# An FFT filter gated with a state-space scan: warm-up, small steps off VectorE, a fifth mirrored pair of row groups, and a new order

## The chip, the cores and the metric

The kernel runs on one core of a Trainium2 chip. The metric is the device time of one execution in microseconds (us), lower is better. Three runs of the kernel before took 306.59 to 307.20 us, with a median of 306.85 us.

A core has five engines that run side by side. TensorE (PE in the profile, and PEld for its weight loads) multiplies matrices into PSUM. VectorE (DVE), ScalarE (ACT) and GpSimd (POOL) do elementwise work, and SyncE (SP) here does nothing but issue DMA transfers. Each engine takes its instructions strictly in the order of its own queue, so an instruction that waits holds back everything behind it.

## The reference

`x` has 2048 rows (positions) of 1024 features. Two branches are computed from it and mixed by a gate of one number per row.

```python
g = sigmoid((x * gate_w).sum(-1, keepdims=True))
a = irfft2(rfft2(x) * (w_r + 1j * w_i))              # over all 2048 x 1024
# b: a diagonal state-space model over the 2048 positions
Lam_bar = exp(dt * Lam);  B_bar = ((Lam_bar - 1) / Lam)[:, None] * Bmat
h[t] = Lam_bar * h[t-1] + B_bar @ x[t]               # 1024 complex states
b = 2 * real(h @ Cmat.T) + x * Dskip
return g * a + (1 - g) * b
```

## The kernel before

**The filter branch** does its Fourier transforms as matrix products. `load_x` brings in `x`, `turn` transposes row groups on TensorE (`pt`, L938, against the permuting identity `ident_g`), `turn_out` copies them to `xQ` (L947), and `fold` adds and subtracts halves on VectorE (`preT`, `sums`, L961 to L972) so that the products that follow are smaller. A row group is a value of `j` from 0 to 15. The first four go one at a time and the other twelve in pairs, which makes the groups n = 0 to 9 of the tuple `MIRROR` (n = 5 is the pair j = 6, 7). In a group that is not mirrored, the forward transform along the features takes four products L445 and four wide ones L455 per row group. In a mirrored group, the odd half is first reversed by one product with an exchange matrix (`ps_r`, L988), VectorE then adds and subtracts it (L994, L995), the even half is split once more (L970, L971, L972 in place of L968), and the transform is made of the narrower products L442, L445 and L451. The results go to DRAM and come back turned (L495, L523), are transformed along the positions (L609), multiplied by the weights on VectorE (`times_w`, L632 to L637), and transformed back (L648, L662, L670, L681, L825, L829, L844 to L865).

The column of frequency zero does not fit into that scheme. `middle` computes it by itself in a chain of about twenty very small steps that pass from engine to engine: `Wrev` (L547), `Bcol` (L562, L563), `Zp` (L572), `Zr` (L577, L582), `Q` (L584 to L587), `Qb` (L590, L591), the product `qps` (L594) and `Qn` (L597). ScalarE writes `Qn` into the first column of each `X2` (L620), which L632 multiplies. `unit_cols` (L625) puts ones into the first column of the weights.

**The scan branch** works in eight chunks of 256 positions. For each, TensorE makes B x into `psu` (L410, 32 products per block of 128 states), ScalarE casts it to `h` (L420), and VectorE does a two-level scan: products with tables of powers (L340, L343), joins (L346, L349), `fold` (L362), the scan instruction itself (L368), then ScalarE scales (L372, into `su` or `xQ`), VectorE adds (L376), and a last pair of products and joins (L340, L343, L383, L387) gives the states. The first two chunks are done in two halves each (`NSEP`), with tiles of half the size and `su` in place of `xQ`. TensorE then makes `ps_y` (L732, and `ps_q` L746 in the last chunk) from `h` and the transposes of C (`CT`, loaded by L721). The tables of powers `tab` are made by `make_tab` in four passes: angles (L281 on ScalarE or L283 on VectorE, chosen per block of states by the tuple `ANG_ACT`), sine and cosine, and casts on all three elementwise engines (L289 to L306).

**The order of the work** is written by hand. Every part is a generator, and each letter of the string `ORDER` advances one of them by one step. `PIECES` gives the order of the pieces of the scans, and `SLOTS` the PSUM buffer of each product. Each engine's queue follows from that. Three more constants matter here. `WARM` is the number of products of zeros (`psw`, L1005) that `keep_warm` puts at the head of TensorE's queue; they need only the tile `idle` (a part of `A1_4`), which VectorE clears (L1000). `FILL_T` says how many transposes of the identity that nobody reads (L936) stand before the transposes of a row group. `ident_g` (L218) is a copy of the identity that the iota-like mask of GpSimd makes.

Of the kernel before, what the change touches and what calls it, by code (L numbers as in the profile page):

```python
# [57 lines left out]
ORDER = (
    "xTUffxxVVTTUGaTffGV2VVVG|far|xaFEUffFfUttxaTTfFSTktxx2TfEUUfttUAfUSAEaTwFEffafTrtfttStUFFEfUtTffbFEA",
    "fSUf~uF2TUEbttxxUUSArU1EASSUAAtSFEFbbbbbttbAtffget~frbEutttbbhHtbftttS1FEbffbtttbAb~tt1t1ut11hHSvAFE",  # L60
    "ftvhH~urrrr1tFF1vStKcEeScccctckf11AvvEtvccvvtthhthvhttthttvcHttetttcct1tAHHHtvvvcfeHFEvwvvvvvSvtvtSv",
    "ttvvvvvvFvvvwvvcccvvvvvvEwcA11hSSA1AK1hAe1KKKKsYsYshsHsHsHhhvvvvvvvMLnWHvvvnvNJnvvvsNJnvvvvssvsvMMvv",
    "sshsvNvYsHLyyNs3hs44vvvvHhWHMvmm+j5535M44MJnMW6nnH3Mvvvm7v7N5vJvv+vn5WvM4N8856hvhvJm4vvJ7vWY+Wvj5H3N",
    "J7vN5H44h56y8v+j8m+YHhM377H8v54ymWn84556vNndvvvhJMvv5M3M5N77nn+5dvhvvvvYy6hvvvv8m+vm445WHJJNNmdM37Mh",
    "87vHJH558+mv44j6v8YMy77n83YX+mJHNnJ8+vv554+y4m56vN5nvY5v5hv768yv7vNvmnvv877v+mvvJHhJH8+8vqhvvYiivmhq",
    "qiii+yvmNIIvqniYHHvIvii+IvIIvvvvvIqJqnqiIvIiIvvm+mNNJJvvvvvnviIivi%nI+vNvvvvvIyvqiIhXYNiivvHIhIlHJlp",
    "phlzJzlZXZPPzzhZZZZHRRHRRRRppZZZZdmyPZo+ROvZvlQQlQoooDzvDmOvvPlQBvvRvBzZZZv++vpOBDDYlOvoZPZZQRRQvRRR",
    "zzRBDvZpPloOlCZDzovZZZOvZoYDzvBBvooYYQZZoZZRZRDQZ9RooDQRRyR9C00yDDD9C99Q09900D00",
# [76 lines left out]
def kernel(  # L145
# [72 lines left out]
    nc.vector.tensor_copy(out=ident_g.rearrange("p (g s) -> p g s", g=2), in_=ident.rearrange("p (s g) -> p g s", g=2))  # L218
# [314 lines left out]
    def middle():  # L533
# [38 lines left out]
        nc.vector.tensor_copy(out=Zp, in_=zps.rearrange("p c b -> p b c"))  # L572
# [50 lines left out]
    def unit_cols():  # L623
        for p in range(4):
            nc.vector.tensor_copy(out=fft["Wb"][p % 2][:, :, :, 0], in_=unit_w.unsqueeze(2).to_broadcast([P, 2, 4]))  # L625
            yield
# [612 lines left out]
```

## Time and profile before

| what | value |
|---|---|
| median of three runs | 306.85 us |
| the profiled execution: time, span | 306.91 us, 305.1 us |
| PE busy, instructions | 294.8 us (97%), 2464 products |
| DVE busy, instructions | 289.2 us (95%), 374 |
| ACT busy, instructions | 207.0 us (68%), 309 |
| POOL busy, instructions | 72.0 us (24%), 106 |
| first product, first copy of `xQ` on VectorE | 1.90 us, 5.65 us |
| last matmul ends, last VectorE instruction ends | 300.34 us, 300.72 us |

The span is what the profiler saw between the first and the last instruction of that execution; 1.8 us of the time lie around it. A row of the groups gives line, engine, operation, tiles and count, then the busy time in us, the mean duration of one in ns, and the idle time of the engine just before these instructions with the engine that ended it. A row of the chain of waits gives the start, the length and the instruction. A row of the timeline gives the start, the busy time, and the engine, followed by the instruction and, in brackets, the idle time ahead of it. A row of the windows gives the busy time of each engine within a stretch of time, and after the letter x the number of instructions.

### The profile page before, as it was taken

How to read it: one execution, taken by the hardware profiler on the slowest of the kernel's cores; microseconds unless marked ns; L12 is line 12 of the kernel's file. 1: busy time of each engine (PE TensorE's matmuls, PEld its weight loads, DVE VectorE, ACT ScalarE, POOL GpSimd, SP SyncE). 2: the span in 40 equal slices, each digit the busy share in tenths (PEclk: the TensorE clock that was granted, in tenths of full speed). 3: DMA queues.
4: the chain of work that ended last, by engine and by line, in shares of the span. 5: the costliest groups of instructions: out<-in, count | busy, mean ns of one | idle time of the engine just before them, and what ended most of it. 6: DMA issues, size and time to landing. Idle time of an engine off the chain costs nothing.

```text
span 305.1 us, 6248 instructions
## 1 busy us (share of the span) xinstructions
PE 294.8 (97%) x2464; PEld 195.4 (64%) x2464; DVE 289.2 (95%) x374; ACT 207.0 (68%) x309; POOL 72.0 (24%) x106
## 2 busy tenths in 40 slices
PE   7989999999999999999999999999999999999993
PEld 4555687886884584467564763688567995465442
DVE  3999999999989999999999999999999999999993
ACT  1699999897541385958886888856979866393200
POOL 1133155393710002110202112120102033351430
PEclk9999999999999999999999999999999999999999
DMA  7999996999994977899989868998659726999796
GB/s 236 367 210 195 202 227 190 105 208 154 217 247 82 259 174 145 201 261 280 212 220 216 213 163 206 236 245 248 179 167 210 145 26 124 156 175 187 104 142 227
DMA packets 74140, 59.21 MB, mean 194 GB/s; under 512 B 44872, under 2 KB 61664, under 8 KB 74112
## 3 DMA queue, kind: packets, MB, share of 16 engines
q1 hardware_dynamic: 66560, 49.69, 64.6%
q0 software_dynamic: 6896, 8.69, 23.2%
q10 hardware_dynamic: 656, 0.44, 0.4%
q8 instruction: 19, 0.31, 0.4%
q14 instruction: 9, 0.07, 0.1%
HBM read 27.33 MB, written 23.08 MB: 165 GB/s over the span
## 4 chain that ended last, share of the span: by engine, by line
PE 68%; DVE 21%; ACT 5%; issue 3%; DMA 2%; POOL 0%; SPq 0%; POOLq 0%; ACTq 0%; DVEq 0%
PE ps_y L732 24%; PE psu L410 23%; PE ps_q L746 7%; DVE h L368 3%; DVE h L343 2%; PE ps_id L829 2%; DVE xQ L947 2%; DMA xs<-in_A_x_dram 2%; DVE UV L632 1%; ACT ZT L690 1%; PE ps_is L681 1%; PE ps_id L825 1%; PE ps_s L474 1%; PE ps_fd L455 1%; PE ps_s L609 1%
## 5 line engine op out<-in xcount | busy, mean ns | idle before, releaser
L410 PE MATMUL psu<-xQ,BT 128*128 128x256 bf16 x1024 | 115.7, 273 | 0.4 <-ACT A_last L489 0.3
L410 PEld LDWEIGHTS <-BT 128*128 128x128 bf16 x1024 | 99.3, 98 | 16.4 <-issue 3.8
L732 PE MATMUL ps_y<-CT,h 128*128 128x512 bf16 x416 | 93.5, 379 | 0.7 <-ACT ye L763 0.4
L732 PEld LDWEIGHTS <-h 128*128 128x128 bf16 x416 | 39.8, 98 | 48.8 <-issue 3.9
L804 POOL DMA_DIRECT2D y_scratch<-su x20 | 17.8, 953 | 127.3 <-ACT su L798 95.3
L420 ACT CAST h<-psu 128x1024 bf16<-128x1024 f32 x32 | 32.1, 1013 | 17.4 <-PE psu L410 12.5
L343 DVE TENSOR_TENSOR h<-h,tab 128x4096 bf16<-128x4096 bf16 (+1 forms) x20 | 37.3, 1863 | 0.6
L368 DVE TENSOR_TENSOR_SCAN h<-rz,h 128x512 bf16<-128x512 f32 (+1 forms) x14 | 36.3, 2617 | 0.2
L763 ACT ACTIVATE ye<-ps_y,omg 128x512 f32<-128x512 f32 x26 | 17.4, 686 | 17.6 <-PE ps_y L732 9.9
L372 ACT ACTIVATE xQ<-h,r_sb 128x254 bf16<-128x254 bf16 x48 | 21.3, 503 | 9.1 <-DVE h L368 9.1
L340 DVE TENSOR_TENSOR xQ<-h,tab 128x4096 bf16<-128x4096 bf16 x12 | 27.4, 2281 | 0.0
L746 PE MATMUL ps_q<-CT,h 128*128 128x512 bf16 (+2 forms) x112 | 20.9, 349 | 0.0
L870 POOL DMA_DIRECT2D BT<-y_scratch x10 | 12.6, 1538 | 27.4 <-issue 23.3
L619 ACT CAST X<-ps_s 128x1024 bf16<-128x1024 f32 x16 | 16.1, 1007 | 4.3 <-PE ps_s L609 2.9
L690 ACT CAST ZT<-ps_is 128x1024 bf16<-128x1024 f32 x16 | 16.9, 1113 | 2.0 <-issue 1.2
L656 ACT CAST C<-ps_is 128x1024 bf16<-128x1024 f32 x16 | 15.6, 1010 | 3.4 <-PE ps_is L648 2.6
L836 ACT ACTIVATE BT<-ps_id,gB 128x1024 bf16<-128x1024 f32 x14 | 15.1, 1111 | 3.6 <-DMA out_dram<-BT 1.8
L746 PEld LDWEIGHTS <-h 128*128 128x128 bf16 x112 | 10.4, 98 | 10.5
L461 ACT CAST X<-ps_fd 128x1024 bf16<-128x1024 f32 x16 | 16.1, 1015 | 0.1
L798 ACT ACTIVATE su<-xs,omg 128x512 f32<-128x512 bf16 x20 | 14.0, 720 | 0.5 <-DVE xs L788 0.5
L372 ACT ACTIVATE su<-h,r_sb 128x254 bf16<-128x254 bf16 x16 | 7.0, 495 | 8.4 <-DVE Zp L572 4.6
L947 DVE COPY xQ<-pt 128x1024 bf16<-128x1024 bf16 x12 | 8.1, 682 | 3.8 <-PE pt L938 3.8
(211 smaller groups left out, 432.9 us busy)
## 6 DMA issues: line engine op xcount, KB each, us to landing
y_scratch<-ye SPq DMA_DIRECT2D x20, 256.0 KB, 2.9
y_scratch<-su POOLq DMA_DIRECT2D x20, 256.0 KB, 6.5
Bb<-turn_scratch SPq DMA_DIRECT2D x16, 256.0 KB, 4.8
turn_scratch<-C SPq DMA_DIRECT2D x16, 256.0 KB, 4.3
raw<-turn_scratch SPq DMA_DIRECT2D x8, 512.0 KB, 5.2
xs<-in_A_x_dram SPq DMA_DIRECT2D x13, 256.0 KB, 5.3
out_dram<-BT SPq DMA_DIRECT2D x11, 256.0 KB, 4.8
CT<-in_A_x_dram SPq DMA_DIRECT2D x5, 512.0 KB, 5.2
```

The source lines that it names most:

```text
L340: nc.vector.tensor_mul(out=tmps["s"], in0=u[:, :, ::-1], in1=bc(i))
L343: nc.vector.tensor_mul(out=u, in0=u, in1=bc(i))
L368: nc.vector.tensor_tensor_scan(out=seg, data0=flat(rz, i), data1=seg, initial=0.0, op0=ALU.mult, op1=ALU.add)
L372: nc.scalar.activation(out=tmps["s"][:, 0, :, i, 1:TS], in_=u[:, 1, :, i, 0:TS - 1], func=ACT.Copy, scale=r2_sb[:, js.start + i:js.start + ...
L410: nc.tensor.matmul(psu[:, j, :], lhsT=BT[4 * q + j][:, ri, d8, :], rhs=xQ[:, c, d8, :], start=(d8 == 0), stop=(d8 == 7))
L420: nc.scalar.copy(out=hs[c][:, :, ri, 4 * q:4 * q + 4].rearrange("p e b (q j) -> p e b q j", j=16), in_=psus.pop((c, q, ri)).rearrange("p b ...
L461: (nc.vector.tensor_copy if j in FD_DVE else nc.scalar.copy)(out=X1.rearrange("p r (m e c) -> p r m e c", e=2, c=2), in_=psf.pop(j).rearra ...
L690: nc.scalar.copy(out=fft["ZT"][:, kp, :, :, 2 * G:2 * G + 2], in_=pszs.pop((G, kp)).rearrange("p v (x n) -> p x n v", n=64))
L732: nc.tensor.matmul(psy, lhsT=hs[c][:, tq, ri, jb, :], rhs=CT[ri][:, jb, 512 * dh:512 * (dh + 1)], start=(i == 0), stop=(i == 15 and tb not ...
L746: nc.tensor.matmul(psq, lhsT=hs[c][:, tq, ri, jb, :], rhs=CT[ri][:, jb, at:at + n], start=(i == 0), stop=(i == 15))
L763: nc.scalar.activation(out=ye, in_=psys[tb][:, K * hf:K * (hf + 1)], func=ACT.Copy, scale=omg[:, tb:tb + 1])
L804: nc.gpsimd.dma_start(out=y_dram[tb, hf], in_=xgs[tb, hf], accum_op=ALU.add)
```

## The change

- `WARM` goes from 7 to 5, and `FILL_T` from 22 to 6 transposes.
- `ident_g` (L218) is copied by GpSimd instead of VectorE.
- All eight angle products of `make_tab` are now on ScalarE (L281); four were on VectorE (L283).
- `MIRROR` takes in group 5, so one more pair of row groups has its odd half mirrored. On TensorE this makes 20 in place of 16 L442, 44 in place of 48 L445, 40 in place of 32 L451, 24 in place of 32 L455, and 5 in place of 4 L988. On VectorE one L968 goes, and one each of L970, L971, L972, L994 and L995 comes.
- In `middle`, six copies (L547, L562, L563, L572, L582, L597) go from VectorE to ScalarE, and five steps (L584, L586, L587, L590, L591) to GpSimd; the four copies of `unit_cols` (L625) go to GpSimd.
- `ORDER`, `PIECES` and `SLOTS` are new, so the instructions of every engine are in another order.

```diff
-FILL_T = {2: 22}
-WARM = 7
+FILL_T = {2: 6}
+WARM = 5
-ANG_ACT = (4, 5, 6, 7)
+ANG_ACT = (0,1,2,3,4,5,6,7,)
-    0, 1, 3, 2, 4, 5, 6, 7, 9, 8, 10, 11, 12, 13, 14, 15, 16, 17, 18, 20, 21, 19, 22, 24, 23, 25, 26, 27, 28, 29, 30,
+    0, 1, 2, 3, 5, 6, 9, 4, 8, 10, 11, 7, 12, 13, 14, 15, 16, 18, 17, 20, 21, 22, 19, 24, 23, 25, 26, 27, 29, 28, 30,
...
-MIRROR = (6, 7, 8, 9)
+MIRROR = (5, 6, 7, 8, 9)
...
-    nc.vector.tensor_copy(out=ident_g.rearrange("p (g s) -> p g s", g=2), in_=ident.rearrange("p (s g) -> p g s", g=2))
+    nc.gpsimd.tensor_copy(out=ident_g.rearrange("p (g s) -> p g s", g=2), in_=ident.rearrange("p (s g) -> p g s", g=2))
...
-        nc.vector.tensor_copy(out=Wrev, in_=wrps)
+        nc.scalar.copy(out=Wrev, in_=wrps)
...
-        nc.vector.tensor_copy(out=Bcol[:, 0:2], in_=aps.rearrange("j (r b a) -> j r a b", r=2, a=4))
-        nc.vector.tensor_scalar_mul(out=Bcol[:, 2], in0=Bcol[:, 0], scalar1=-1.0)
+        nc.scalar.copy(out=Bcol[:, 0:2], in_=aps.rearrange("j (r b a) -> j r a b", r=2, a=4))
+        nc.scalar.activation(out=Bcol[:, 2], in_=Bcol[:, 0], func=ACT.Copy, scale=-1.0)
...
-        nc.vector.tensor_copy(out=Zp, in_=zps.rearrange("p c b -> p b c"))
+        nc.scalar.copy(out=Zp, in_=zps.rearrange("p c b -> p b c"))
...
-        nc.vector.tensor_copy(out=Zr[:, 0], in_=zrp[:, :, 0])
-        nc.vector.tensor_mul(out=Q[:, 0], in0=each(AB[:, 0]), in1=every(Zp.rearrange("p b r -> p r b")))
-        nc.vector.tensor_mul(out=Q[:, 1], in0=each(AB[:, 1]), in1=every(Zr))
-        nc.vector.tensor_add(out=Q[:, 0], in0=Q[:, 0], in1=Q[:, 1])
+        nc.scalar.copy(out=Zr[:, 0], in_=zrp[:, :, 0])
+        nc.gpsimd.tensor_mul(out=Q[:, 0], in0=each(AB[:, 0]), in1=every(Zp.rearrange("p b r -> p r b")))
+        nc.gpsimd.tensor_mul(out=Q[:, 1], in0=each(AB[:, 1]), in1=every(Zr))
+        nc.gpsimd.tensor_add(out=Q[:, 0], in0=Q[:, 0], in1=Q[:, 1])
...
-        nc.vector.tensor_sub(out=Qb[:, :, 0], in0=Q[:, 0, 0, 0], in1=Q[:, 0, 1, 1])
-        nc.vector.tensor_add(out=Qb[:, :, 1], in0=Q[:, 0, 1, 0], in1=Q[:, 0, 0, 1])
+        nc.gpsimd.tensor_sub(out=Qb[:, :, 0], in0=Q[:, 0, 0, 0], in1=Q[:, 0, 1, 1])
+        nc.gpsimd.tensor_add(out=Qb[:, :, 1], in0=Q[:, 0, 1, 0], in1=Q[:, 0, 0, 1])
...
-        nc.vector.tensor_copy(out=Qn.rearrange("p b r -> p (b r)"), in_=qps)
+        nc.scalar.copy(out=Qn.rearrange("p b r -> p (b r)"), in_=qps)
...
-            nc.vector.tensor_copy(out=fft["Wb"][p % 2][:, :, :, 0], in_=unit_w.unsqueeze(2).to_broadcast([P, 2, 4]))
+            nc.gpsimd.tensor_copy(out=fft["Wb"][p % 2][:, :, :, 0], in_=unit_w.unsqueeze(2).to_broadcast([P, 2, 4]))
```

The new order is seen at three places. The first is VectorE's queue at the third of the four half chunks of the scan, from its scan L368 to its L376, which adds what ScalarE makes of that scan, and a little on. Before:

```order
L362 TENSOR_TENSOR h<-h 128x2x512
L368 SCALAR_TENSOR_TENSOR h<-rz,h 128x512 x2
L380 TENSOR_TENSOR ck<-h,rot 128x4x4
L547 COPY Wrev<-Wrev_ps 128x64
L562 COPY Bcol<-aps 32x128
L563 TENSOR_SCALAR Bcol<-Bcol 32x64
L376 TENSOR_TENSOR h<-h,su 128x2x512
```

And with the change:

```order
L380 TENSOR_TENSOR ck<-h,rot 128x4x4
L340 TENSOR_TENSOR xQ<-h,tab 128x4096
L376 TENSOR_TENSOR h<-h,su 128x2x512
L343 TENSOR_TENSOR h<-h,tab 128x4096
L349 TENSOR_TENSOR h<-xQ,h 128x2x1024
```

Three small steps of `middle` have left the stretch between the scan and its L376, and the first wide product of a whole chunk (L340 into `xQ`) stands there instead.

The second place is GpSimd's queue around the first store of `su` (L804, an accumulating DMA into the scratch array of the output), where the five steps of `Q` and `Qb` and the first two copies of `unit_cols` now stand. Before, it read:

```order
L550 TENSOR_TENSOR Wh<-Wc,Wrev 128x32
L551 TENSOR_TENSOR Wh<-Wc,Wrev 128x32
L554 TENSOR_TENSOR AB<-Wh 128x32
L555 TENSOR_TENSOR AB<-Wh 128x32
L556 TENSOR_SCALAR AB<-AB 128x64
L804 DMA y_scratch<-su 128x512 x18
```

And with the change:

```order
L556 TENSOR_SCALAR AB<-AB 128x64
L625 COPY Wb<-unit_w 128x8
L804 DMA y_scratch<-su 128x512
L584 TENSOR_TENSOR Q<-AB,Zp 128x64
L586 TENSOR_TENSOR Q<-AB,Zr 128x64
L587 TENSOR_TENSOR Q<-Q 128x64
L590 TENSOR_TENSOR Qb<-Q 128x16
L591 TENSOR_TENSOR Qb<-Q 128x16
L804 DMA y_scratch<-su 128x512 x2
L625 COPY raw<-unit_w 128x8
```

The steps of `Q` and `Qb` now stand behind one L804, which waits for an L798 of ScalarE and for a store of `ye` to land.

The third place is SyncE's queue at the loads of C (L721), and the stores of the forward transform (L495) of the tiles `A1` (A_129), `A1_last` and `A1_sc`. Before:

```order
L721 DMA_TRANSPOSE CT_82<-in_B_C_re_dram 128x8x128
L495 DMA turn_scratch<-A_129 128x2x512
L721 DMA_TRANSPOSE CT_83<-in_B_C_im_dram 128x8x128
L721 DMA_TRANSPOSE CT_82<-in_B_C_re_dram 128x8x128
L721 DMA_TRANSPOSE CT_83<-in_B_C_im_dram 128x8x128
L721 DMA_TRANSPOSE CT_82<-in_B_C_re_dram 128x8x128
L721 DMA_TRANSPOSE CT_83<-in_B_C_im_dram 128x8x128
L495 DMA turn_scratch<-A_129 128x2x512
L495 DMA turn_scratch<-A_last 128x2x512 x2
L495 DMA turn_scratch<-A_sc 128x2x512 x2
```

And with the change, to the end of these loads:

```order
L495 DMA turn_scratch<-A_last 128x2x512 x2
L721 DMA_TRANSPOSE CT_82<-in_B_C_re_dram 128x8x128
L721 DMA_TRANSPOSE CT_83<-in_B_C_im_dram 128x8x128
L721 DMA_TRANSPOSE CT_82<-in_B_C_re_dram 128x8x128
L721 DMA_TRANSPOSE CT_83<-in_B_C_im_dram 128x8x128
L495 DMA turn_scratch<-A_sc 128x2x512
L721 DMA_TRANSPOSE CT_82<-in_B_C_re_dram 128x8x128
L721 DMA_TRANSPOSE CT_83<-in_B_C_im_dram 128x8x128
L721 DMA_TRANSPOSE CT_82<-in_B_C_re_dram 128x8x128
L721 DMA_TRANSPOSE CT_83<-in_B_C_im_dram 128x8x128
L721 DMA_TRANSPOSE CT_82<-in_B_C_re_dram 128x8x128
L721 DMA_TRANSPOSE CT_83<-in_B_C_im_dram 128x8x128
L495 DMA turn_scratch<-A_sc 128x2x512
```

All sixteen loads of C stood ahead of the last five stores; now ten of the loads stand behind the stores of `A1_last`, and six of them behind the first store of `A1_sc` as well.

More of the change, by code (lines that the diff above doesn't have):

```diff
@@ L44 @@
 PIECES = (
[7 rows of a table removed]
[7 rows of a table added]
 )
 SLOTS = (
-    "0123012320132012012310210321032103201230132013201302310231012312032103131201203103203013031203120312",
-    "0312310210321021321032320310321032032031031023102310210321230120310321032",
+    "0123012310231012301230123013201320123012301202130213023102310231023102320132013320120132130132130130",
+    "13012010123012301301302302130213021301302132132310231023123103210321230123",
 )
-MIRROR = (6, 7, 8, 9)
+MIRROR = (5, 6, 7, 8, 9)
 ORDER = (
[L59 to L68, printed above, removed]
@@ new lines @@
+    "xxTU2TxffUGGVVVVVfVGaxx|aaffT22xUfTttffU|ffFFtTTEaaETtUttFkSaxEfTUxtfFTAUffSUExttfArfUbbrbtbTFSS~bFT",
+    "fUErTfuUUUUUUttfFrtbfbtbAAttFtSEESErSgAAffbffbASAhbtt~~etHuhutbFFttttttttFtffHvtwEEEbbbbSFEftttvv11t",
+    "wh~uhr1ttSSShvtKeHAFF1H1t1tArAA111ctvftt11vt~vcHfvEhhtuvfEt1vvvSttStcctHHvAAtccFFvt1vvEEvrhHvevvvv1t",
+    "SSvvchcKhhvtttvvveKKccAhvA1vnvvccwewKcvvvcvcc1KsHYshvvHHvHvWnWvvvvvvNJvvNMJnnYMvvssvvvvvvNvYssLvvyvv",
+    "vvvvvNHLJvjhHshsHssksvvmmhWW3+yHvvmnsssss44vJY+ynnvMMMM3+vN5vnvvNv5JJ5vvm4Ym645M7vMhNN73vhJj5W45y46H",
@@ new lines @@
+    "v8875vJ8MM+h3vv75H+mv458Mn6Mh4HNYW78v5v3m557Jvj8nH44vv65vMn+vvM77535Nh44vv68M8v7y+5Wmn7JNh3v55vh88HW",
+    "N6Hv+4m4HmvJYnXj7M3Jvh78544N8HvY556vJyv7++7m5mvd88+nNn55678vvN7Jvhvv+8vYdqnhHvNvHJiyvqmmIvviIvqvvhHq",
+    "++viivhIIYiiHvvvvyqymvvvIIiIqnJvvmiiqIIviIv+v+nNNvvmmivqiJnJviIivInviIIvYvYidyhNI%+yIlvhXXvvvvvzlvHJ",
+    "NHJpzPpPdZZ+hlllZZZmhZQQH+zRRvRRRzZZRZppRHDoDZRmvYlpPPZZQOovvlzvzlOvDQZBZovZZBvRRZZQQPvzDzRRvloZOvZp",
+    "vDoOoRZlZBRvDDZvBooZQDzOvvvzZZvvBOBQoPZZRoZZoRDDCYoRR90yRR90CyY+99DQDC9900oQD0090Y",
```

12 rows, old and new, of the table PIECES are left out of this document.

## The prediction

> **What bounds the kernel now.** I read the busy shares of the page first, then the windows of 10 us, then the chain of waits, and last the groups, shapes apart, for the prices.
>
> ```profile
> span 305.1 us, 6248 instructions
> PE 294.8 (97%) x2464; PEld 195.4 (64%) x2464; DVE 289.2 (95%) x374; ACT 207.0 (68%) x309; POOL 72.0 (24%) x106
> ```
>
> Both TensorE and VectorE are busy nearly all the time, so the share alone doesn't say which of them sets the end.
>
> ```profile
> core 0: us, PE busy (x) PEld busy (x) DVE busy (x) ACT busy (x) POOL busy (x), PEclk, DMA share, GB/s
> 0.00:10.00 10.00, 8.11 (x77) 5.42 (x78) 4.72 (x19) 2.22 (x7) 1.90 (x13) 1.00 0.81 270
> 20.00:30.00 10.00, 9.68 (x75) 4.96 (x76) 9.90 (x23) 9.81 (x13) 4.71 (x6) 1.00 1.14 206
> 80.00:90.00 10.00, 10.00 (x94) 8.72 (x92) 8.60 (x15) 4.69 (x7) 3.56 (x10) 1.00 0.91 225
> 210.00:220.00 10.00, 9.24 (x82) 5.95 (x81) 9.86 (x9) 9.49 (x15) 0.86 (x1) 1.00 0.63 176
> ```
>
> VectorE idles 5.3 us in the first stretch and 1.4 us at 80 to 90 us; in the other stretches shown it is 9.9 of 10 busy, and what is missing there is the step from one instruction to a dependent one. TensorE shows holes where it waits for the others, as at 210 to 220 us. A matmul that is queued behind another counts as busy, so its 97% is an upper value.
>
> ```profile
> 1.33 0.35 DVE ident_g L218
> 1.90 3.17 PE psw L1005 x7
> 5.07 0.56 PE pt L938 x8
> 5.65 0.70 DVE xQ L947
> 211.42 1.81 ACT h L420 x2
> 279.57 20.77 PE ps_q L746 x112
> 300.37 0.35 DVE raw L918
> ```
>
> The chain starts on VectorE with a copy that the throwaway products don't need but stand behind, passes through those products, and hands VectorE its first real work at 5.65 us. Around 211 us it goes from VectorE's scan through ScalarE to TensorE again, and it ends in TensorE's last products, whose inputs VectorE finished. So VectorE's queue, with no slack after 5.65 us, sets the joins, and TensorE runs from join to join with little slack of its own.
>
> **The change part by part.** The start comes first. `ident_g` leaves VectorE, so the clearing of `idle` begins right away and not after 1.33 us; five products at 3.17 / 7 = 0.45 us take 2.3 us and end near 3.3 us.
>
> ```profile
> 1.00 0.29 POOL masks.py:199 TENSOR_SCALAR_AFFINE_SELECT ident<-ident 128x128 bf16<-128x128 bf16 x1
> 0.73 1.35 SPq L247 DMA_DIRECT2D CT<-in_A_x_dram  x3
> CT<-in_A_x_dram SPq DMA_DIRECT2D x2, 256.0 KB, 2.8
> ```
>
> The identity ends at 1.29 us, and even a copy that GpSimd takes a whole microsecond for would have `ident_g` ready by 2.4 us. The first tile of `x`, issued at 0.73 us, lands 2.8 us later, at 3.5 us. From there to VectorE the chain above has 0.56 us, or 0.8 us from the first of the eight transposes if they run slowly, so VectorE begins at 4.1 to 4.5 us in place of 5.65 us. **Term one: -1.2 us**, with bounds of 0 (the second tile of `x` lands late) and -1.5.
>
> Next comes VectorE's work.
>
> ```profile
> L283 DVE TENSOR_SCALAR ang<-tau_f,ang 128x256 f32<-128x256 f32 x4 | 1.2, 343 | 0.0
> L572 DVE CAST Zp<-zps 128x32 bf16<-128x32 f32 x1 | 0.2, 162 | 0.0
> L625 DVE COPY Wb<-unit_w 128x8 bf16<-128x8 bf16 x2 | 0.4, 176 | 0.0
> L994 DVE TENSOR_TENSOR preT<-preT,ps_r 128x512 bf16<-128x512 bf16 x4 | 2.7, 680 | 0.2 <-PE ps_r L988 0.2
> L995 DVE TENSOR_TENSOR preT<-preT,ps_r 128x512 bf16<-128x512 bf16 x4 | 2.7, 687 | 0.1
> L970 DVE TENSOR_TENSOR sums<-sums 128x512 bf16<-128x512 bf16 x4 | 1.9, 483 | 0.1
> L971 DVE TENSOR_TENSOR preT<-sums 128x256 bf16<-128x256 bf16 x4 | 1.2, 292 | 0.1
> L972 DVE TENSOR_TENSOR preT<-sums 128x256 bf16<-128x256 bf16 x4 | 1.1, 282 | 0.0
> L968 DVE TENSOR_TENSOR preT<-sums 128x512 bf16<-128x512 bf16 x2 | 0.8, 416 | 0.0
> ```
>
> It loses four L283 (1.2), six copies that go to ScalarE (0.16 us for L572, 1.2 together with the slightly larger others), five steps of that kind that go to GpSimd (1.0 together) and four L625 (0.7): 4.1 us. The mirrored pair adds 0.68 + 0.69 + 0.48 + 0.29 + 0.28 and takes off one L968 of 0.42: 2.0 us. By durations that is -2.1 us, but short instructions overlap their neighbours, so I take **term two: -1.7 us**, bounds -1.2 and -2.1.
>
> The third term is the hole at 80 to 90 us, which is a wait for ScalarE.
>
> ```profile
> DVE h L376 <- ACT su L372: 1.6, 2, 1.1
> 85.74 1.70 ACT L372 ACTIVATE su<-h,r_sb 128x254 bf16<-128x254 bf16 x4 [1.10 <-DVE h L368]
> L340 DVE TENSOR_TENSOR xQ<-h,tab 128x4096 bf16<-128x4096 bf16 x12 | 27.4, 2281 | 0.0
> ```
>
> ScalarE needs 1.7 us between a scan and its L376. Before, only the small steps covered it; in the new order a 2.28 us L340 stands there. **Term three: -1.0 us** of the 1.6, bounds 0 (ScalarE is late with its own queue) and -1.6.
>
> What moves must be paid elsewhere. ScalarE takes four angle products of 0.5 us and six copies of about 0.2 us, 3.2 us in all.
>
> ```profile
> L281 ACT ACTIVATE ang<-tau_f,ang 128x256 f32<-128x256 f32 x4 | 1.8, 502 | 0.0
> ```
>
> In the first 70 us ScalarE is as full as VectorE (9.81 of 10 at 20 to 30 us), and its late casts are what TensorE and VectorE would then wait for; after that it has room (4.69 of 10 at 80 to 90 us). I put this, with the joins that VectorE now reaches earlier, into the next term.
>
> TensorE must keep up.
>
> ```profile
> L936 PE MATMUL pt<-ident 128*128 128x128 bf16 x22 | 1.4, 219 | 0.0
> L455 PE MATMUL ps_fd<-G_sb,preT 128*128 128x512 bf16 x32 | 8.2, 379 | 0.0
> L451 PE MATMUL ps_fd<-G_sb,preT 128*128 128x256 bf16 x32 | 4.8, 272 | 0.0
> L988 PE MATMUL ps_r<-preT,JP_sb 128*128 128x512 bf16 x4 | 1.5, 384 | 0.0
> ```
>
> Its first transposes start at 3.5 in place of 4.86 us (-1.4, the two products included), 16 identity transposes go (16/22 of 1.4 = -1.0), and the mirrored pair exchanges eight L455 (8.2/32 each) for eight L451 (4.8/32 each) and one L988: -0.5. That is -2.9 us of a queue that the chain shows to end at 300.34 us, if its own stalls stay: 297.4 us. The last L918 then takes 0.35 us, and the span lasts 305.1 - 300.72 = 4.4 us beyond that one: a bound of 302.2 us. VectorE's three terms alone would give 305.1 - 3.9 = 301.2 us. **Term four: +1.2 us** for the two engines meeting at tighter joins, bounds 0 and +2.5. Sum: 305.1 - 1.2 - 1.7 - 1.0 + 1.2 = 302.4 us of span, and with 1.8 us around it **304.2 us**. The profiled execution is 0.06 us above the median, which I neglect.
>
> The loads of C are the transfer at risk.
>
> ```profile
> 80.68 1.32 SPq L721 DMA_TRANSPOSE CT<-in_B_C_im_dram  x1
> CT<-in_B_C_im_dram SPq DMA_TRANSPOSE x8, 6.0
> 90.69 10.52 PE L732 MATMUL ps_y<-CT,h 128*128 128x512 bf16 x48
> ```
>
> The last one is issued at 80.7 us, takes 6.0 us to land at the median, and TensorE uses the tile from 90.7 us: 4 us to spare. Behind the stores of `A1_last` and `A1_sc`, which wait for ScalarE, I estimate from the places in the queues that the last issue comes 4 to 5 us later, and that TensorE reads the half it fills about 1 us later than the first: hidden by about a microsecond.
>
> Two rules of the Trainium skill speak against parts of this. For the start: the seven products went at 0.45 us each, where a product of that width takes 10.52 / 48 = 0.22 us later on, so the front runs at half pace although the granted clock reads 1.00 in the first window. The Trainium skill, "TensorE: Matmul & The Clock Gate" (Part 1), says that the clock opens only after a busy window of about 3.4 us that runs freely, and Part 4 that transposes don't count as busy in the same way; by that, the shorter warm-up could leave what follows at half pace for one more window. The trace, where the pace changed after 3.2 us of products, agrees so far. Rival (e) prices it from rows.
>
> For the steps on GpSimd, the rows are these (from the timeline):
>
> ```profile
> 78.27 1.23 DVE L340 TENSOR_TENSOR su<-h,tab 128x2048 bf16<-128x2048 bf16 x1
> 78.41 1.16 POOL L1035 TENSOR_SCALAR omg_bf<-g_bf 128x16 bf16<-128x16 bf16 x1
> 79.54 1.23 DVE L343 TENSOR_TENSOR h<-h,tab 128x2048 bf16<-128x2048 bf16 x1
> ```
>
> A GpSimd instruction of sixteen elements lasts 1.16 us and ends as the VectorE product ends that it began beside. The Trainium skill, "SBUF — State Buffer" (SBUF: two separate sides), says that the two engines share a pair of ports, which one takes for a whole instruction while the other stands still, VectorE with two inputs in SBUF included. By that rule the nine steps moved to GpSimd are not free: each may wait for a VectorE instruction or hold one up. Rival (b) rests on the row alone.
>
> **The rivals.** (a) TensorE takes it all back: VectorE is early, but TensorE's stalls at the joins grow by what VectorE saved, because the new order leaves less between the end of a chunk on VectorE and its first `ps_y`. For it, TensorE is as full as VectorE; against it, TensorE loses 2.9 us of work too. Then term four is +3.0 and the time 306.0 us, between 305.6 and 306.9. (b) Slower: the chain of `Q` and `Qb` on GpSimd. By my count of the queues it stands behind an L804 that is issued at about 111 us; five dependent steps, each held up by a VectorE instruction of 1.2 to 2.3 us, as L1035 above by L340, end at 112.5 us undisturbed and at 118 to 122 us if each is held up. TensorE reaches `qps` at about 116.5 us and stops there, and VectorE's L632, due at about 120.5 us, waits for `Qn` and two casts. Below 117 us nothing shows; from about 120 us on the gain is gone; at 122 us the time is 304.2 + 4.5 = 308.7 us. Against it: the 4.4 us scan L368 falls there, and one hold-up would cover several steps only if they slip in between. (c) The same on the other side: the waits of TensorE shrink too (the windows lack 0.3 us of it at 20 to 30 us and 0.8 us at 210 to 220 us), so that term four is 0 or a little less: 302.6 us. (d) C lands late: 2 us later than I estimate, TensorE and the joins lose 1 us, 305.2 us. (e) Half pace for longer in front: the eight transposes of the first tile take twice their 0.56 us, and the next tile's are hidden only in part: +0.9, 305.1 us.
>
> **How the numbers follow.** The forecast, 303.4 to 305.5 us, gets 0.48, with (d) and (e) inside it at 0.05 each; (a) 0.22; (b) 0.14; (c) 0.16. The range from 302.4 to 307.3 us leaves out the far ends of (b) and (c). A measurement here tells no change from 0.2% (0.6 us), so 306.24 and 307.46 us are the bounds. Faster takes the forecast, (c) and half of (a): 0.74. The same takes most of the rest of (a) and the low part of (b): 0.13. Slower is the rest of (b) and the tail of all: 0.13.
>
> **What would show it.** Right: VectorE's first L947 starts at 4.2 to 4.5 us; its busy time falls by about 2 us; L376's wait for `su` falls below 0.6 us; VectorE's last L918 ends near 298 us. Wrong: an L732 that waits for CT near 91 us, L632 or `qps` idle near 117 to 121 us, L586 to L591 on GpSimd lasting a microsecond each, or TensorE's idle time at the joins above the 10 us that the page now shows as missing from its span.

## The result, and the profile after

The changed kernel took 308.79 us (median of four runs, 308.29 to 309.04), and the kernel before, measured beside it, 306.94 us (306.59 to 307.20). The ratio is 1.0059, with a 95% interval of 1.0041 to 1.0077: slower by 0.6%, where I had forecast 304.2 us, and outside the range that ended at 307.3 us. The profiled execution of the changed kernel took 308.29 us, with a span of 306.5 us.

The page of the changed kernel, which answers to the two rows shown of before:

```profile
span 306.5 us, 6239 instructions
PE 295.4 (96%) x2447; PEld 195.6 (64%) x2447; DVE 287.6 (94%) x358; ACT 209.6 (68%) x319; POOL 86.8 (28%) x116
```

VectorE is busy for 1.6 us less, close to the 1.7 us of the sum. GpSimd is busy for 14.8 us more, far more than the nine small steps lasted on VectorE (1.7 us). The windows of 10 us of the changed kernel show where the time went (the columns are those of the windows before):

```profile
core 0: us, PE busy (x) PEld busy (x) DVE busy (x) ACT busy (x) POOL busy (x), PEclk, DMA share, GB/s
0.00:10.00 10.00, 7.88 (x58) 5.00 (x59) 5.44 (x21) 3.37 (x7) 1.70 (x10) 1.00 0.77 256
80.00:90.00 10.00, 10.00 (x80) 7.42 (x79) 9.78 (x12) 3.63 (x6) 0.00 (x0) 1.00 1.02 188
110.00:120.00 10.00, 7.43 (x63) 4.46 (x61) 10.00 (x7) 4.95 (x9) 7.57 (x5) 1.00 0.79 174
120.00:130.00 10.00, 8.28 (x28) 3.22 (x28) 4.83 (x3) 5.34 (x12) 3.61 (x5) 0.66 0.53 93
```

The start and the stretch from 80 to 90 us did what was forecast: VectorE is 0.7 us busier in the first and 1.2 us busier in the second. The loss is at 110 to 130 us, where next to nothing was lost before:

```profile
110.00:120.00 10.00, 10.00 (x89) 7.01 (x87) 9.81 (x11) 7.75 (x13) 1.86 (x2) 1.00 0.67 135
120.00:130.00 10.00, 10.00 (x74) 4.07 (x73) 9.96 (x6) 7.84 (x16) 0.86 (x1) 1.00 0.91 212
```

With the change, TensorE stands still for a time, VectorE idles for 5.2 us, and the granted clock falls to 0.66 on average in the second of these windows. The waits of the changed kernel name the place:

```profile
PE qps L594 <- POOL Qb L591: 4.3, 1, 4.3
DVE UV L632 <- POOL raw L625: 3.1, 1, 3.1
DVE h L376 <- ACT xQ L372: 2.5, 2, 2.2
```

This is rival (b). The timeline of the changed kernel shows its mechanism, GpSimd's five steps beside VectorE's instructions:

```profile
111.67 4.42 DVE L368 TENSOR_TENSOR_SCAN h<-rz,h 128x2048 bf16<-128x2048 f32 x1
112.28 0.96 POOL L804 DMA_DIRECT2D y_scratch<-su  x1 [11.17 <-ACT su L798]
112.98 3.23 POOL L584 TENSOR_TENSOR Q<-AB,Zp 128x64 f32<-128x64 f32 x1
116.01 2.35 DVE L340 TENSOR_TENSOR xQ<-h,tab 128x4096 bf16<-128x4096 bf16 x1
116.18 2.35 POOL L586 TENSOR_TENSOR Q<-AB,Zr 128x64 f32<-128x64 f32 x1
118.28 0.80 DVE L788 TENSOR_TENSOR xs<-xs,Db 128x1024 bf16<-128x1024 bf16 x1
118.61 0.65 POOL L587 TENSOR_TENSOR Q<-Q 128x64 f32<-128x64 f32 x1
119.00 2.40 DVE L343 TENSOR_TENSOR h<-h,tab 128x4096 bf16<-128x4096 bf16 x1
119.34 2.15 POOL L590 TENSOR_TENSOR Qb<-Q 128x16 bf16<-128x16 f32 x1
121.45 0.22 POOL L591 TENSOR_TENSOR Qb<-Q 128x16 bf16<-128x16 f32 x1
121.72 0.19 PE L594 MATMUL qps<-Qb,KRS_sb 128*128 128x32 bf16 x1 [4.29 <-POOL Qb L591]
121.94 0.19 ACT L597 CAST Qn<-qps 128x32 bf16<-128x32 f32 x1 [3.70 <-PE qps L594]
124.21 0.20 ACT L620 COPY X<-Qn 128x2 bf16<-128x2 bf16 x1
124.50 2.29 DVE L632 TENSOR_TENSOR UV<-X,Wb 128x4096 bf16<-128x4096 bf16 x1 [3.09 <-POOL raw L625]
```

The first four steps of 64 or 16 elements end within 0.2 us of the end of the VectorE instruction that they began beside: 116.21 with the scan (116.09), 118.53 with the L340 (118.36), 119.26 with the L788 (119.08), 121.49 with the L343 (121.40). The chain takes 8.7 us. TensorE, which reached `qps` at 117.4 us, waits until 121.7. Then `Qn`, two casts and two copies of the column follow on ScalarE, and VectorE's L632 starts at 124.5 us. The profile puts that wait down to L625, but the last thing before it is ScalarE's second L620, which ends at 124.4 us. A second wait of VectorE follows at 127.9 us: L376 stands for 2.2 us until L372 is done, and the clock has a part in it, as is shown below.

### The profile page after: what moved, and what is told of

It reads as the page before. It is cut to its first block, busy times and chain, and to the rows that moved or that the text cites. A ratio compares the mean times of both kernels' runs of the same rounds, so it can differ in the third digit from the quotient of the medians.

```text
span 306.5 us, 6239 instructions
## 1 busy us (share of the span) xinstructions
PE 295.4 (96%) x2447; PEld 195.6 (64%) x2447; DVE 287.6 (94%) x358; ACT 209.6 (68%) x319; POOL 86.8 (28%) x116
## 4 chain that ended last, share of the span: by engine, by line
PE 46%; DVE 42%; DMA 5%; ACT 3%; issue 2%; SPq 1%; DVEq 0%; POOL 0%; ACTq 0%
PE ps_y L732 14%; PE psu L410 14%; PE ps_q L746 7%; DVE h L343 6%; DVE h L368 5%; DVE UV L632 4%; DVE su L340 3%; DVE xQ L340 3%; PE ps_id L829 2%; DMA Bb<-turn_scratch 2%; DMA y_scratch<-su 2%; DVE xQ L947 2%; DVE h L383 2%; DVE h L349 2%; DVE h L362 2%
## 5 line engine op out<-in xcount | busy, mean ns | idle before, releaser
L732 PE MATMUL ps_y<-CT,h 128*128 128x512 bf16 x416 | 95.9, 386 | 0.0
L732 PEld LDWEIGHTS <-h 128*128 128x128 bf16 x416 | 40.4, 99 | 54.0 <-issue 10.8
L804 POOL DMA_DIRECT2D y_scratch<-su x20 | 19.5, 1035 | 73.9 <-ACT su L798 73.9
L343 DVE TENSOR_TENSOR h<-h,tab 128x4096 bf16<-128x4096 bf16 (+1 forms) x20 | 37.6, 1883 | 0.5
L368 DVE TENSOR_TENSOR_SCAN h<-rz,h 128x512 bf16<-128x512 f32 (+1 forms) x14 | 36.0, 2596 | 0.2
L763 ACT ACTIVATE ye<-ps_y,omg 128x512 f32<-128x512 f32 x26 | 17.6, 692 | 21.3 <-PE ps_y L732 17.1
L340 DVE TENSOR_TENSOR xQ<-h,tab 128x4096 bf16<-128x4096 bf16 x12 | 27.5, 2293 | 0.4 <-ACT h L420 0.3
L372 ACT ACTIVATE xQ<-h,r_sb 128x254 bf16<-128x254 bf16 x48 | 21.0, 512 | 3.5 <-DVE h L368 3.5
L798 ACT ACTIVATE su<-xs,omg 128x512 f32<-128x512 bf16 x20 | 14.3, 728 | 1.3 <-DMA y_scratch<-su 1.1
L632 DVE TENSOR_TENSOR UV<-X,Wb 128x4096 bf16<-128x4096 bf16 x4 | 9.2, 2291 | 4.7 <-POOL raw L625 3.1
L289 POOL CAST tab<-sc 128x512 bf16<-128x512 f32 x4 | 3.7, 921 | 28.9 <-ACT sc L1136 28.9
```

Of the source, the lines that this page charges most:

```text
L340: nc.vector.tensor_mul(out=tmps["s"], in0=u[:, :, ::-1], in1=bc(i))
L343: nc.vector.tensor_mul(out=u, in0=u, in1=bc(i))
L368: nc.vector.tensor_tensor_scan(out=seg, data0=flat(rz, i), data1=seg, initial=0.0, op0=ALU.mult, op1=ALU.add)
L372: nc.scalar.activation(out=tmps["s"][:, 0, :, i, 1:TS], in_=u[:, 1, :, i, 0:TS - 1], func=ACT.Copy, scale=r2_sb[:, js.start + i:js.start + ...
L632: nc.vector.tensor_mul(out=UV, in0=X2s.pop(g).unsqueeze(1).to_broadcast([P, 2, 2, 2, K]), in1=W.unsqueeze(2).to_broadcast([P, 2, 2, 2, K]))
L732: nc.tensor.matmul(psy, lhsT=hs[c][:, tq, ri, jb, :], rhs=CT[ri][:, jb, 512 * dh:512 * (dh + 1)], start=(i == 0), stop=(i == 15 and tb not ...
```

## The experiments

### Undoing one part of the chain's move, in two steps

In the first, all five steps go back to VectorE, where they fall right behind the scan L368.

```diff
-        nc.gpsimd.tensor_mul(out=Q[:, 0], in0=each(AB[:, 0]), in1=every(Zp.rearrange("p b r -> p r b")))
+        nc.vector.tensor_mul(out=Q[:, 0], in0=each(AB[:, 0]), in1=every(Zp.rearrange("p b r -> p r b")))
...
-        nc.gpsimd.tensor_sub(out=Qb[:, :, 0], in0=Q[:, 0, 0, 0], in1=Q[:, 0, 1, 1])
-        nc.gpsimd.tensor_add(out=Qb[:, :, 1], in0=Q[:, 0, 1, 0], in1=Q[:, 0, 0, 1])
+        nc.vector.tensor_sub(out=Qb[:, :, 0], in0=Q[:, 0, 0, 0], in1=Q[:, 0, 1, 1])
+        nc.vector.tensor_add(out=Qb[:, :, 1], in0=Q[:, 0, 1, 0], in1=Q[:, 0, 0, 1])
```

> The changed kernel with the five steps of Q and Qb (L584, L586, L587, L590, L591) back on VectorE; they fall between the scan L368 that ends at 116.1 us and the next L340. Theory A (this chain, held up on GpSimd, made the loss): the chain ends near 117.2 us in place of 121.7, TensorE's wait at qps falls from 4.3 to under 0.5 us, the granted clock stays at 1.00 from 118 to 126 us in place of 0.50, VectorE's idle time at 122 to 130 us (5 us) goes, VectorE does 1.0 us more work, and the time is 303.5 to 305.5 us. Theory B (the loss sits in tighter joins all along, and would come back at the next one): the wait at qps goes but the time stays above 307 us.

It took 302.67 us (301.60 to 303.06), at a ratio to the kernel before on the same chip of 0.9843 (0.9803 to 0.9883). The time fell even below the 303.5 to 305.5 us of theory A, and theory B falls. From its timeline, and the window of 120 to 130 us:

```profile
115.89 0.20 DVE L584 TENSOR_TENSOR Q<-AB,Zp 128x64 f32<-128x64 f32 x1
116.61 0.17 DVE L591 TENSOR_TENSOR Qb<-Q 128x16 bf16<-128x16 f32 x1
117.17 0.18 PE L594 MATMUL qps<-Qb,KRS_sb 128*128 128x32 bf16 x1
```

```profile
120.00:130.00 10.00, 9.84 (x78) 4.55 (x78) 10.00 (x9) 8.84 (x18) 3.53 (x3) 1.00 0.81 194
```

On VectorE the chain takes 0.9 us, not 8.7, `qps` doesn't wait, and both engines are full again. VectorE's busy time over the whole kernel is 287.7 us, against 287.6 us with the five steps on GpSimd: moving steps of 1.0 us away had saved VectorE 0.1 us. Some of its instructions beside them had been longer (L788 0.80 us against 0.68 here, L343 2.40 against 2.28).

In the second step only the three steps of `Q` are on VectorE, and the two of `Qb` stay on GpSimd.

```diff
...
-        nc.gpsimd.tensor_mul(out=Q[:, 1], in0=each(AB[:, 1]), in1=every(Zr))
-        nc.gpsimd.tensor_add(out=Q[:, 0], in0=Q[:, 0], in1=Q[:, 1])
+        nc.vector.tensor_mul(out=Q[:, 1], in0=each(AB[:, 1]), in1=every(Zr))
+        nc.vector.tensor_add(out=Q[:, 0], in0=Q[:, 0], in1=Q[:, 1])
```

> Three of the five steps (L584, L586, L587) on VectorE, the two of Qb (L590, L591) on GpSimd. Theory A: L590 is held up by the one VectorE instruction beside it (the 2.3 us L340), so Qb ends near 119.4 us, TensorE waits about 2 us at qps, its clock stays at 1.00 since the idle time is too short to close it, and the time lies about 2 us above that of the kernel with all five on VectorE, at 305.5 to 307. Theory B: no difference between the two, both above 307 us.

It took 304.68 us (303.74 to 307.41), ratio 0.9908 (0.9881 to 0.9935): 2.0 us above the first, as theory A has it, though the two intervals still touch. The time itself came out 0.8 us below the forecast range, as that of the first step did. The lines are of the slowest of its eight executions (307.41 us), the only one with a trace:

```profile
116.73 2.28 DVE L340 TENSOR_TENSOR xQ<-h,tab 128x4096 bf16<-128x4096 bf16 x1
116.90 2.20 POOL L590 TENSOR_TENSOR Qb<-Q 128x16 bf16<-128x16 f32 x1 [3.46 <-DVE Q L587]
119.07 0.66 POOL L591 TENSOR_TENSOR Qb<-Q 128x16 bf16<-128x16 f32 x1
119.78 0.18 PE L594 MATMUL qps<-Qb,KRS_sb 128*128 128x32 bf16 x1 [2.12 <-POOL Qb L591]
```

A step of 16 elements lasts as long as the L340 beside it, and TensorE waits 2.1 us. So it matters how many of the steps are on GpSimd: none, two and five of them give 302.7, 304.7 and 308.8 us.

### Held up, or slow by themselves

Here the five steps stay on GpSimd, but stand ahead of the first L804 there.

```diff
 ORDER:
-HshsHssksvvmmhWW3+yHvvmnsssss44
+HshsHsskssssvvmmhWW3+yHvvmnss44
```

The letter `s` advances the first-column chain by a step, and `+` the stores L804.

> The changed kernel with the five steps on GpSimd, but ahead of the first L804 in its queue; every other queue is as in the changed kernel. Theory A1 (GpSimd is held up by VectorE's instructions with two inputs): L584 starts at about 107.6 us and ends with a VectorE instruction, L586 waits for Zr at 111 us and is then held up, at the latest by the 4.4 us scan from 111.7 to 116.1; the last step ends at 117.5 to 121 us, and the time lies between 305 and 308.5 us. Theory A2 (these steps are slow on GpSimd by themselves, with the durations 3.2, 2.4, 0.7, 2.2 and 0.2 us that the changed kernel showed): L584 is over by 111 us and the rest ends at 111 + 5.4 = 116.4 us, TensorE does not wait at qps, and the time is 303 to 305 us. Which of the two holds is read from the ends: by A1 each step ends within 0.15 us of the end of a VectorE instruction, by A2 the durations repeat.

```profile
107.65 1.23 DVE L343 TENSOR_TENSOR h<-h,tab 128x2048 bf16<-128x2048 bf16 x1
107.81 1.25 POOL L584 TENSOR_TENSOR Q<-AB,Zp 128x64 f32<-128x64 f32 x1 [6.65 <-ACT Zp L572]
111.12 0.40 POOL L586 TENSOR_TENSOR Q<-AB,Zr 128x64 f32<-128x64 f32 x1 [2.07 <-ACT Zr L582]
111.60 0.65 POOL L587 TENSOR_TENSOR Q<-Q 128x64 f32<-128x64 f32 x1
111.99 4.53 DVE L368 TENSOR_TENSOR_SCAN h<-rz,h 128x2048 bf16<-128x2048 f32 x1
112.32 4.22 POOL L590 TENSOR_TENSOR Qb<-Q 128x16 bf16<-128x16 f32 x1
116.50 2.29 POOL L591 TENSOR_TENSOR Qb<-Q 128x16 bf16<-128x16 f32 x1
123.76 0.17 ACT L597 CAST Qn<-qps 128x32 bf16<-128x32 f32 x1
```

The durations don't repeat. L584 takes 1.25 us where it took 3.23, L586 0.40 where it took 2.35, L590 4.22 where it took 2.15, and L591 2.29 where it took 0.22, each according to the VectorE instruction beside it. The steps end up to 0.19 us behind those instructions, a little more than the 0.15 us that I had set. A1 holds and A2 falls. TensorE's wait at `qps` shrinks to 1.3 us, but the time is 306.82 us (305.98 to 307.46), ratio 0.9983 (0.9964 to 1.0003), since a new wait has taken its place: the product is done at 119.0 us, and ScalarE makes `Qn` only at 123.8 us. In ScalarE's queue `Qn` stands behind an L798 whose buffer the delayed store L804 has to free first. I had not seen that when I wrote the expectation, so it is luck that the time fell within it.

### TensorE's part and VectorE's part

In the next kernel the chain stays as in the change, and only `qps` stands sixteen products later in TensorE's queue.

```diff
 ORDER:
-yHvvmnsssss44vJY+ynnvMMMM3+vN5
+yHvvmnsssvJY+ynss44nvMMMM3+vN5
```

> The changed kernel with the product qps placed sixteen products of ps_y (3.5 us) later in TensorE's queue; the queues of GpSimd and ScalarE are the same. Qb still ends near 121.5 us. Theory A-PE (what hurts is TensorE standing still, and its clock closing): TensorE waits under 1 us, the clock stays at 1.00, TensorE gains 3.5 us of work and some 2.8 us of half pace, and the time falls to 303 to 306 us. Theory A-DVE (what hurts is VectorE waiting for Qn at L632, 3.1 us, and behind it for L376, 2.2 us): Qn is there no earlier, VectorE's idle time at 120 to 130 us stays at 5 us, and the time stays above 307.5 us.

It took 305.37 us (304.76 to 306.50), ratio 0.9944 (0.9922 to 0.9966). `Qb` comes at 121.4 us as before, TensorE waits 0.8 us, and the granted clock stays at 1.00. VectorE still starts L632 at 124.3 us, after an idle time of 3.1 us, as theory A-DVE had it, but the time falls by 3.4 us all the same. So neither theory holds alone: 3.4 of the 6.1 us between the change and the kernel with the chain on VectorE came back when `qps` stood later in TensorE's queue. What is left, 2.7 us, still has VectorE's wait of 3.1 us for `Qn` and TensorE's of 0.8 us in it, and no run parts these two.

The other kernel keeps TensorE's queue and gives it something to do while it waits: 64 throwaway products of the identity by itself, written into the tile of `qps` before `qps` is.

```diff
-        qps = psum([P, 32], "qps")
+        qps = psum([P, P], "qps")
+        for _ in range(64):
+            nc.tensor.matmul(qps, lhsT=ident, rhs=ident, start=True, stop=True)
...
```

> The changed kernel with 64 throwaway products of 128 columns (identity by identity, 3.6 us at full pace) just ahead of qps in TensorE's queue, where it otherwise stands still for 4.3 us; Q and Qb stay on GpSimd. Qb comes at 121.5 us as before. If the closing of the clock (half pace from 121 to 126.4 us) is a cost of its own, TensorE's row at 120 to 130 us shows a clock of 1.00, the first two ps_y after qps take 7.0 in place of 9.4 us, and the time falls by 1.5 to 2.5 us to 306.3 to 307.3. If the half pace was hidden by VectorE's wait for Qn, the time stays within 0.5 us of 308.8.

It took 306.24 us (305.73 to 306.99), ratio 0.9972 (0.9955 to 0.9989): 2.55 us less than the change, with `Qb`, `qps` and L632 at the same times. In the line numbers of this kernel, where L634 is the former L632 and L734 the former L732 (the last line is a window of 10 us):

```profile
117.29 3.74 PE L595 MATMUL qps<-ident 128*128 128x128 bf16 x64
121.74 0.18 PE L596 MATMUL qps<-Qb,KRS_sb 128*128 128x32 bf16 x1 [0.71 <-POOL Qb L591]
121.98 6.85 PE L734 MATMUL ps_y<-CT,h 128*128 128x512 bf16 x31
124.51 2.29 DVE L634 TENSOR_TENSOR UV<-X,Wb 128x4096 bf16<-128x4096 bf16 x1 [3.08 <-POOL raw L627]
120.00:130.00 10.00, 9.17 (x70) 4.42 (x70) 6.92 (x6) 7.21 (x15) 4.46 (x6) 1.00 0.63 122
```

The products after the wait take 6.85 us here, and in the change 9.5 us for one more of them. In the change's windows the granted clock is 1.00 until 119 us, 0.97 in the next microsecond, 0.50 from 120 to 126, 0.81 on average from 126 to 128, and 1.00 again:

```profile
119.00:120.00 1.00, 0.00 (x0) 0.00 (x0) 1.00 (x2) 0.00 (x0) 0.92 (x2) 0.97 1.00 221
120.00:121.00 1.00, 0.00 (x0) 0.00 (x0) 1.00 (x1) 0.00 (x0) 1.00 (x1) 0.50 0.74 168
121.80:124.00 2.20, 2.20 (x7) 0.79 (x7) 0.00 (x0) 2.02 (x4) 1.81 (x3) 0.50 0.54 61
124.00:126.00 2.00, 2.00 (x7) 0.62 (x5) 1.50 (x1) 1.18 (x4) 0.00 (x0) 0.50 1.03 142
```

So the clock closed during the wait of 4.3 us, and the half pace after it cost 2.55 us of its own. The way to VectorE leads through ScalarE, whose L763 waits for the slow `ps_y` and holds back the L372 behind it, for which VectorE's L376 then stands 2.2 us:

```profile
127.87 0.69 ACT L763 ACTIVATE ye<-ps_y,omg 128x512 f32<-128x512 f32 x1 [2.65 <-PE ps_y L732]
```

With the 64 products the waits of all L376 together are down from 2.5 to 0.5 us. The Trainium skill, "TensorE: Matmul & The Clock Gate" (Part 1), lets about 3.4 us without work bring half rate back. The trace shows the same effect sooner: the clock fell at 120.0 us, some 2.5 us after TensorE had stopped at 117.4. With two of the steps on GpSimd, where TensorE waits 2.1 us (from 117.7 to 119.8 us), I had expected the clock to stay open. In the profiled execution it did not, as a window of 1 us shows:

```profile
121.00:122.00 1.00, 1.00 (x4) 0.31 (x3) 0.86 (x1) 0.97 (x3) 0.94 (x2) 0.50 1.27 119
```

The granted clock is 1.00 up to 120, 0.58 in the next microsecond, 0.50 to 123, 0.72 to 124, and 1.00 again: some 3 us at half pace followed a wait of 2.1 us. That is shorter than the page's figure, and the measurement decides here. But it is not so each time. Over the whole kernel the mean granted clock was 0.993 in this execution and 0.994 in the next slowest (305.65 us), and 0.999 or 1.000 in the other six (303.74 to 305.07 us), so in most of them the clock seems to have stayed open, as expected. After the waits of 1.3 and 1.5 us in the trace of the kernel with the steps ahead of the first L804 (at `qps` and at the next `ps_y`) it stayed at 1.00. Where the bound lies, and what moves it from run to run, is open. Nor does a shorter half pace always show in the time: of the change's own four executions one had a mean clock of 0.994 and not 0.989, and took 308.59 us.

### The same move in the old order

Is it the move or the place? Here the kernel before has its five steps on GpSimd and nothing else is changed.

> The kernel before with one thing changed: the five steps of Q and Qb on GpSimd, ahead of the first L804 there. If VectorE's instructions hold the steps up in this order too, each ends with a VectorE instruction, Qb comes at about 109 to 111 us in place of 107.7, VectorE (whose Qn, L597, stands ahead of an L340) and TensorE wait 1 to 3 us, and the time is 307 to 309 us. If the steps are as quick there as the small steps L550 to L556 (0.25 us each at 86 to 87 us), VectorE saves 1.0 us and the time is 305.9 to 306.9 us.

It took 307.33 us (306.92 to 307.90), ratio 1.0005 (0.9993 to 1.0017): no change, at the low end of what the first theory gave and above the second.

```profile
106.86 0.68 DVE L376 TENSOR_TENSOR h<-h,su 128x1024 bf16<-128x1024 bf16 x1
107.02 0.70 POOL L586 TENSOR_TENSOR Q<-AB,Zr 128x64 f32<-128x64 f32 x1 [1.54 <-DVE Zr L582]
109.53 0.19 DVE L597 CAST Qn<-qps 128x32 bf16<-128x32 f32 x1 [0.53 <-PE qps L594]
```

The steps are held up here too, L586, L587 and L590 by instructions of some 0.7 us, so `Qb` comes about 1.5 us later than before, at 109.3 us. VectorE waits 0.5 us for it. It is rid of 1.0 us of steps, but its busy time stays at 289.2 us, and the time shows no gain. Here as in the change, what is left of the VectorE instruction that happens to run beside a step is its price.

### What the other parts are worth

With the chain on VectorE as the base (302.67 us, ratio 0.9843), one part at a time was undone.

```diff
 f1: front
-FILL_T = {2: 6}
-WARM = 5
+FILL_T = {2: 22}
+WARM = 7
-    nc.gpsimd.tensor_copy(out=ident_g...
+    nc.vector.tensor_copy(out=ident_g...
 f2: angles
-ANG_ACT = (0,1,2,3,4,5,6,7,)
+ANG_ACT = (4, 5, 6, 7)
 f3: the six copies of middle
-        nc.scalar.copy(out=Wrev, in_=wrps)
+        nc.vector.tensor_copy(out=Wrev, in_=wrps)
...
 g1: all of these, and L625, at once
 g3: the fifth mirrored pair
-MIRROR = (5, 6, 7, 8, 9)
+MIRROR = (6, 7, 8, 9)
```

For g3 the two letters of `ORDER` that reverse and fold group 5 and its place in `SLOTS` go as well.

> The changed kernel with Q and Qb on VectorE (the base of this set: 302.7 us), and its front undone: seven products, 22 identity transposes, ident_g copied by VectorE. If VectorE's start sets the time (the prediction's term one), its first L947 moves back by about 1.0 us to 5.6 us and the time rises by 0.8 to 1.5 us, to 303.5 to 304.2. If the start is taken up by the first waits for ScalarE or for transfers, the time stays within 0.4 us of the base.

> The base with four of the eight angle products back on VectorE (L283). If VectorE's work counts for what its durations say, the time rises by 1.2 us to 303.9. If ScalarE, which is 9.4 to 9.9 of 10 busy from 10 to 60 us in the changed kernel, is what the front waits for, the 2.0 us that it is relieved of make the time fall or stay, 301.5 to 302.9.

> The base with the six small copies of the first-column chain (L547, L562, L563, L572, L582, L597) back on VectorE. By VectorE's durations the time rises by 1.2 us, or some 0.8 us where they overlap their neighbours, to 303.5 to 303.9. A rival: on VectorE they stand behind wide instructions and come later than on ScalarE, so that the product qps waits again; then TensorE's wait there is over 0.5 us and the rise is larger, 2 us or more. Without either, no change within 0.4 us.

> The new order and the fifth mirrored pair with every step on the engine that it had before, and the old front (Q, Qb, the six copies, L625, four angles and ident_g on VectorE, seven products, 22 transposes). The three undone by themselves above the base (302.7 us) cost 0.6 for the front, 0.4 for the angles and 0.9 for the copies. If they add up, the time is 304.6 to 305.2 us, and the rest of the distance to the kernel before, some 2 us, is the new order's. If the order had been made for the new places and is of no use without them, the time is 306 us or more.

> The base (Q and Qb on VectorE, 302.7 us) without the fifth mirrored pair: VectorE does 2.0 us less, TensorE 0.5 us more. If VectorE sets the time throughout, it falls to 300.7 to 301.7 us. If TensorE sets it in the stretch where the pair falls (the first 30 us), or the two share it, the time is 302.5 to 303.5 us.

| kernel | time, us | ratio to before, 95% interval |
|---|---|---|
| base: all of the change, Q and Qb on VectorE | 302.67 | 0.9843 (0.9803 to 0.9883) |
| f1: front undone | 303.29 | 0.9861 (0.9838 to 0.9885) |
| f2: angles undone | 303.06 | 0.9863 (0.9841 to 0.9885) |
| f3: six copies undone | 303.53 | 0.9879 (0.9858 to 0.9900) |
| g3: fifth mirrored pair undone | 302.92 | 0.9874 (0.9849 to 0.9899) |
| g1: every place and the front undone | 305.78 | 0.9965 (0.9948 to 0.9983) |

Each part undone by itself raises the median by 0.3 to 0.9 us, and the interval of each ratio overlaps that of the base, so none of the four is shown by itself. The forecasts were met for f3 (its first case) and g3 (its second); f1 and f2 came out between their two cases. All places together are shown: g1 lies 3.1 us above the base with no overlap, which is more than the 1.9 us that f1 to f3 add up to. The missing 1.2 us may be L625, or what single parts hide from each other, or noise, since 0.9 us couldn't be told from nothing above; that wasn't tried. Of the forecast for g1 the lower case, with adding up, was missed by 0.6 us, and the other case, in which the order is of no use without the places, was just short of its bound. The new order and the fifth pair alone are worth 0.35% (0.17 to 0.52) against the kernel before.

The fifth pair takes 2.0 us of VectorE's time and gives TensorE 0.5 us, and undoing it doesn't lower the time. In its trace VectorE does work 1.4 us less than the base (286.3 to 287.7 us), but waits for TensorE, 1.2 us at a copy of `turn_out` at 24 us and 1.0 us at the start of a fold at 40 us:

```profile
DVE preT L960 <- PE ps_fd L450: 1.0, 1, 1.0
DVE xQ L946 <- PE pt L937: 4.8, 2, 3.6
```

(L960 and L946 of this kernel are L961 and L947 of the others; the other 3.6 of the second row's 4.8 us are the start.) That VectorE sets the time throughout, which the forecast of 300.7 to 301.7 us rested on, does not hold at these two places.

## Why the prediction was wrong

**What bounds the kernel.** The reading that two full engines run from join to join held, and it is what made the loss so large: a late chain at one place stopped both. The reading that VectorE alone sets the joins did not hold at 24 and 40 us (g3).

**Term one** (-1.2 us): VectorE's first L947 starts at 4.68 us in place of 5.65, -0.97 us, where I had -1.2. The first transposes ran slowly: the chain of waits of the changed kernel has them at

```profile
3.60 1.05 PE pt L938 x8
4.68 0.70 DVE xQ L947
```

1.05 us for eight, twice the 0.56 us of before. So the half pace of rival (e) was there, and cost 0.5 us in place of 0.9. With the front undone (f1) the first L947 moves back to 5.95 us, but the time rises by only 0.6 us, within the noise of its comparison.

**Term two** (-1.7 us): VectorE's busy time fell by 1.6 us, as forecast, but not wholly for the reason given. Of it the five steps of `Q` and `Qb`, which the sum counts at 1.0 us, were worth 0.1 us: with them back on VectorE it is busy for 287.7 us in place of 287.6.

**Term three** (-1.0 us): L376's wait for `su` went from 1.6 us to nothing that the waits list, so it was -1.6 us, at the end of its bounds. (The 2.5 us of L376 in the waits of the changed kernel are for `xQ`, and belong to the loss at 120 to 130 us.)

**Term four** (+1.2 us): too large without the chain. With the chain on VectorE, which the sum would price at 304.2 + 1.0 us, the time is 302.67 us, 4.2 us below the 306.85 us of before; terms one to three as measured (1.0, 1.5 and 1.6 us) make 4.1 of them, so about nothing is left for term four. The engines met with less loss than I had assumed, close to rival (c).

**The step that failed** is the price of the five steps on GpSimd. The sum put their delay at nothing and left it to rival (b); measured, it is 6.1 us (308.79 us against 302.67 with the steps on VectorE). The mechanism and the place were written down there: steps on GpSimd held up by VectorE's instructions, `Qb` at 118 to 122 us (measured 121.7), TensorE stopped at `qps`, and L632 late. That its 308.7 us at the far end is also the measured time is luck: it was 304.2 + 4.5, and what came was 302.67 + 6.1, with a half pace that rival (b) did not have. I gave (b) 0.14 because the scan of 4.4 us falls there, so that one hold-up might cover several steps if they "slip in between". The trace shows the opposite: L584 began 1.3 us into the scan and was held for the rest of it, and the next three steps were held by one VectorE instruction each; only the last, L591, took its 0.22 us. The row that should have settled it stood in the prediction: an instruction of 16 elements lasted 1.16 us beside a product of 1.23 us. A chain of them, in a stretch where VectorE has no gaps, costs the lengths of the instructions beside them, 4.4 + 2.3 + 0.7 + 2.4 us less the 1.3 us of the scan that had run already; that sum could have been made from the new order and gives 8.5 us, where 8.7 were measured. It belonged in the forecast and not among the rivals. The Trainium skill, "SBUF — State Buffer" (SBUF: two separate sides), said it in one sentence: each of the two engines can hold up the other for a whole instruction. The runs with none and with two of the steps on GpSimd, and the one with the steps ahead of the first L804, agree with it. That the ports are what the steps wait for is the page's reading; the runs show only that they wait.

**What I did not see** is the clock in the middle of the kernel. Rival (e) had it only in the front. Of the 3.4 us that came back when `qps` stood later in TensorE's queue, 2.55 us came back as well when TensorE was only kept busy during the wait. So most of what the wait cost by way of TensorE was the half pace after it, and the 4.3 us of standing still itself 0.9 us, which is within the noise of the two runs.

**Rivals (a) and (d)** did not come. TensorE's listed waits outside this place shrank from 5.3 to 3.4 us, and no L732 waited for C near 91 us.

**The version that is faster than both** is the change with the five steps on VectorE: 302.67 us, a ratio of 0.9843 (0.9803 to 0.9883) to the kernel before.
